# Batches 2 to 7 without TensorE transposes in a windowed attention and gated MLP kernel

## The chip, the cores and the metric

The kernel runs on one core of a Trainium2 chip. The metric is the time of one execution on the device in microseconds, lower is better. The core has TensorE (PE in the profile), VectorE (DVE), ScalarE (ACT), GpSimd (POOL) and SyncE (SP), which here only issues DMAs. Matrix products go from SBUF into PSUM, which has eight banks of 128 partitions x 512 f32.

## What is computed

An attention with a causal window of 64 positions, whose output feeds a gated MLP. Eight batches, eight heads, 576 positions, 64 dimensions a head; everything comes and goes in f32:

```python
scores = scale * np.matmul(q, k.transpose(0, 1, 3, 2))          # q, k, v: (8, 8, 576, 64)
mask = (rel >= 0) & (rel < 64)                                  # rel = query - key
attn = softmax(np.where(mask, scores, -1e9))
x = np.matmul(attn, v)                                          # heads side by side: (8, 576, 512)

h = np.maximum(x @ w_in, 0.0)                                   # (8, 576, 1024)
u, v = h[..., :512], h[..., 512:]
v_n = (v - mean(v)) / np.sqrt(var(v) + 1e-06)
v_s = np.einsum('ts,bsd->btd', w_spatial, v_n) + b_spatial[None, :, None]
out = (u * v_s) @ w_out                                         # (8, 576, 512)
```

## The kernel before

Each batch is cut into small operations with a one-letter name, a batch and an index. `T` transposes q and k on PE, `S` makes scores, `P` multiplies the exponentials by v and by ones (the denominators), `V` and `U` are the two halves of `x @ w_in`, `G` is the product with `w_spatial`, `O` the one with `w_out`. `S2.1` is the scores of batch 2 for heads 2 and 3; index 4 stands everywhere for the remainder, positions 512 to 575 of all eight heads. Between them stand operations of other engines: exponentials, logarithms, relu and output copies on ACT, mask, normalisation and gating on DVE, casts to f16 on POOL and ACT.

`work()` lists all operations with what they depend on and which buffers they take. `RINGS` gives the number of buffers of each kind: `mm` is six PSUM banks shared by all products, `sc` one pair of banks for the scores of two heads, `stg` twelve staging tiles of 128 x 576 f32 into which all loads go. `plan()` lays the operations out: PE takes them in the order written out by hand in `ORDER`, the other engines and the DMA queue by due times that follow from ORDER and from the list `SHIFT`, with the durations in `COST`. What comes out is a fixed program: each engine runs its instructions in that order and waits with semaphores. All DMAs are issued by SP, in one queue.

The scores need q and k with the 64 dimensions of a head on the partitions, while in memory each position has its 64 dimensions in a row. `PATH = "LLRRRRBB"` gives each batch one of three ways to turn them:

- L (batches 0 and 1): one load of two heads, a cast, transposes of 64x64 on PE (L634), evacuation of the bank (L640).
- R (batches 2 to 5): loads of 128 positions of all heads (L664, L667, the rest in L702), casts on POOL (L677, L707), transposes of 128x128 on PE (`emit_T`, L728, L723), evacuation on DVE (L735, L737, L741). `emit_S` (L757, remainder L770) then multiplies with 64 dimensions on 64 rows of PE, four tiles of 64x64 for two heads.
- B (batches 6 and 7): loads of four heads in rows of 2304 bytes (L647), DVE transposes blocks of 32x32 in f32 (L651), and ACT and POOL cast and put the positions in order (L659). Each head lies on 32 partitions in two halves of 32 dimensions. `emit_S2` (L792) adds the two halves up in PSUM, two heads at a time.

Loads of q and k of path R move rows of 256 bytes (64 dimensions of one position of one head), but q of batch 2 rows of 1 KB (`RUN4`). Those of v move rows of 256 bytes in every batch (L681, remainder L711); POOL casts v (L691) and copies it a second time shifted by 64 positions (L696, L697). Output tiles go out through L933 and the remainders through L936.

Of the kernel before, what the change touches and what calls it, by code (L numbers as in the profile page):

```python
# [33 lines left out]
class Op:  # L34
# [11 lines left out]
WINDOW = {"PE": 0, "ACT": 27.5, "DVE": 92.1, "POOL": 361.6, "DMA": 10.0}  # L46
RINGS = dict(stg=12, tt=3, qT=2, kT=2, v16=3, qk=5, rf=1, qkr=2, sc=1, mm=6, e2=3, e2r=2, lnz=2, zinv=2,
# [10 lines left out]
    "loadL": ("DMA", 880, 3050), "DT": ("DVE", 700, 800), "castLP": ("POOL", 1240, 1340), "castLA": ("ACT", 1210, 1340), "S2": ("PE", 450, 670), "S2r": ("PE", 140, 360), "E2r": ("ACT", 320, 450),  # L58
# [31 lines left out]
U6.0 V6.0 P7.0 V6.4 S7.2 G5.4 V6.1 V6.2 S7.4a P7.1 O4.4 S7.3 U6.4 U6.3 U6.1 U6.2 S7.4b P7.2 P7.3 G6.3 G6.0 P7.4 G6.2  # L90
U7.0 G6.1 G6.4 V7.2 U7.1 U7.2 V7.4 O5.4 V7.1 O5.1 V7.0 V7.3 O5.2 O6.0 O5.0 U7.4 O6.1 O5.3 G7.0 U7.3 O6.3 G7.1 G7.3
G7.4 G7.2 O6.4 O7.4 O7.0 O7.2 O7.1 O7.3 O6.2
# [220 lines left out]

PATH = "LLRRRRBB"
RUN4 = {"q": 3, "k": 2}

CAST_P, EVAC_P, CAST_L = "PAPAPAPA", "DADADADA", "APAPAPAP"
# [668 lines left out]
```

## Time and profile before

| | |
|---|---|
| median of 3 runs | 215.63 us (215.62 to 215.91) |
| the profiled execution | 215.76 us |
| its span, first to last instruction | 213.9 us |
| PE, DVE, ACT, POOL busy | 203.4, 163.6, 164.5, 109.8 us |
| DMA queue of SP, share of 16 engines | 77.1% |
| granted PE clock | 1.00 |

Busy time is the union of an engine's instructions; PE's are pipelined, so that the mean duration of a matmul is longer than its share of the time. In the slices of the page each digit is the busy share of 1/40 of the span in tenths. The chain is the work that ended last, followed back from the end. In the stretches each row gives start and end, the length, then busy time and instructions of PE, PEld (weight loads), DVE, ACT and POOL, the granted clock, the busy share of the DMA engines and GB/s. In the groups, after the bar: busy us, mean ns of one, idle time before them and what ended it.

### The profile page before, as it was taken

The numbers are of one execution on the slowest core, as the hardware profiler recorded it, in microseconds if no ns is written. First come the engines' busy times: TensorE is split into PE (matmuls) and PEld (weight loads), VectorE is DVE, ScalarE is ACT, GpSimd is POOL, SyncE is SP. The second block draws the span as 40 slices with busy tenths as digits, with TensorE's granted clock in tenths as the row PEclk, the third lists the DMA queues.
The fourth block names the chain that finished last, engine by engine and source line by source line (L and its number), as shares of the span: only waits on it lengthen the run. The fifth ranks groups of instructions, "written<-read, shape, count | busy, mean of one in ns | idle before, by whom it ended". The sixth has DMA issues, their size and how long they took to land.

```text
span 213.9 us, 7152 instructions
## 1 busy us (share of the span) xinstructions
PE 203.4 (95%) x2921; PEld 113.6 (53%) x2921; DVE 163.6 (76%) x314; ACT 164.5 (77%) x304; POOL 109.8 (51%) x162
## 2 busy tenths in 40 slices
PE   7798989899999999999999999999989999999991
PEld 2544736446645765565664556454555655545540
DVE  6388889678987889778899999996987796546310
ACT  3488889895798589857989979999878797377242
POOL 2546549757689676879726692279992000000000
PEclk9999999999999999999999999999999999999999
DMA  6998999999999998999999999897910100013516
GB/s 181 361 259 280 384 235 239 183 218 291 249 199 208 196 180 199 204 227 203 208 275 260 246 359 356 190 298 241 252 71 8 24 21 8 3 32 140 196 42 255
DMA packets 86387, 42.69 MB, mean 200 GB/s; under 512 B 72465, under 2 KB 76561, under 8 KB 86354
## 3 DMA queue, kind: packets, MB, share of 16 engines
q1 hardware_dynamic: 86354, 42.24, 77.1%
q8 instruction: 23, 0.38, 0.8%
q14 instruction: 10, 0.08, 0.2%
HBM read 32.79 MB, written 9.44 MB: 197 GB/s over the span
## 4 chain that ended last, share of the span: by engine, by line
PE 80%; ACT 6%; DMA 5%; DVE 4%; POOL 2%; issue 1%; SPq 1%
PE pg L905 19%; PE po L918 12%; PE pv L850 12%; PE pu L888 12%; DMA spk<-in_k_dram 5%; PE z L819 4%; PE o L826 4%; PE tp L728 3%; PE sc L757 3%; DVE vn L881 3%; PE pu L892 2%; PE po L922 2%; PE pv L853 2%; PE sc_None L792 2%; POOL kp L627 1%; ACT e L776 1%
## 5 line engine op out<-in xcount | busy, mean ns | idle before, releaser
L905 PE MATMUL pg<-wspT,vn 128*128 128x64 f16 (+1 forms) x256 | 38.8, 287 | 0.7 <-DVE vn L881 0.7
L850 PE MATMUL pv<-win,x 128*128 128x512 f16 x128 | 31.6, 380 | 1.0 <-issue 1.0
L868 DVE BATCH_NORM_STATS2 st<-vs 128x6 f32<-128x512 f16 (+1 forms) x40 | 27.0, 676 | 7.0 <-ACT vs L860 5.1
L888 PE MATMUL pu<-x,win 128*128 128x512 f16 x128 | 32.0, 380 | 0.3 <-ACT win L594 0.2
L691 POOL CAST v<-sv 128x512 f16<-128x512 f32 x32 | 22.3, 699 | 18.9 <-DMA sv<-in_v_dram 18.0
L912 DVE TENSOR_TENSOR g<-pg,ru 128x512 f16<-128x512 f32 (+1 forms) x40 | 24.6, 626 | 9.4 <-PE pg L905 7.1
L776 ACT ACTIVATE e<-sc 128x1024 f16<-128x1024 f32 (+1 forms) x36 | 28.4, 817 | 3.4 <-PE sc L757 1.9
L918 PE MATMUL po<-wout,g 128*128 128x512 f16 x128 | 30.8, 380 | 0.0
L839 DVE TENSOR_TENSOR x<-o,zi 128x512 f16<-128x512 f32 (+1 forms) x40 | 24.6, 629 | 7.8 <-ACT zi L835 7.7
L928 ACT COPY ob<-po 128x512 f32<-128x512 f32 (+1 forms) x40 | 21.6, 543 | 10.5 <-PE po L918 6.3
L808 DVE TENSOR_TENSOR e<-e,mask 128x1024 f16<-128x1024 f16 x32 | 24.4, 765 | 5.8 <-ACT e L776 3.8
L898 ACT ACTIVATE ru<-pu 128x512 f32<-128x512 f32 (+1 forms) x40 | 21.7, 558 | 7.8 <-PE pu L888 5.8
L905 PEld LDWEIGHTS <-vn 128*128 128x128 f16 x256 | 16.8, 98 | 14.6 <-DVE vn L881 0.8
L860 ACT ACTIVATE vs<-pv 128x512 f16<-128x512 f32 x32 | 18.9, 602 | 6.9 <-PE pv L850 6.6
L835 ACT ACTIVATE zi<-ln 128x512 f32<-128x512 f32 (+1 forms) x40 | 22.5, 595 | 0.3
L831 ACT ACTIVATE ln<-z 128x512 f32<-128x512 f32 x32 | 18.3, 607 | 5.2 <-PE z L819 5.0
L697 POOL COPY v<-v 64x512 f16<-64x512 f16 x28 | 19.9, 710 | 1.5
L918 PEld LDWEIGHTS <-g 128*128 128x128 f16 x128 | 11.9, 98 | 13.4 <-issue 0.2
L888 PEld LDWEIGHTS <-win 128*128 128x128 f16 x128 | 11.4, 98 | 13.7 <-ACT win L594 0.7
L850 PEld LDWEIGHTS <-x 128*128 128x128 f16 x128 | 11.6, 98 | 12.8 <-issue 0.6
L905 PE MATMUL pg<-wspT,vnr 128*128 128x64 f16 (+1 forms) x64 | 17.0, 287 | 0.4 <-DVE vnr L881 0.4
L826 PEld LDWEIGHTS <-v 128*64 128x64 f16 x576 | 15.0, 112 | 4.3 <-POOL v L715 0.6
(114 smaller groups left out, 352.7 us busy)
## 6 DMA issues: line engine op xcount, KB each, us to landing
sv<-in_v_dram SPq DMA_DIRECT2D x32, 256.0 KB, 5.5
out_dram<-ob SPq DMA_DIRECT2D x32, 256.0 KB, 3.3
sk<-in_k_dram SPq DMA_DIRECT2D x16, 256.0 KB, 5.6
sq<-in_q_dram SPq DMA_DIRECT2D x16, 256.0 KB, 5.2
spk<-in_k_dram SPq DMA_DIRECT2D x8, 288.0 KB, 5.2
spq<-in_q_dram SPq DMA_DIRECT2D x8, 288.0 KB, 5.6
slk<-in_k_dram SPq DMA_DIRECT2D x8, 288.0 KB, 4.5
slq<-in_q_dram SPq DMA_DIRECT2D x8, 288.0 KB, 5.8
```

Of the source, the lines that this page charges most:

```text
L691: self.nc.gpsimd.tensor_copy(v16[:, 0, n, :, :], s[:, 0:512].rearrange("c (h d) -> c h d", h=8))
L776: self.nc.scalar.activation(to, of, AF.Exp, bias=0.0, scale=0.125)
L808: self.nc.vector.tensor_tensor(e2[:, :, :], e2[:, :, :], m, ALU.min)
L826: mm(o[64 * h:64 * h + 64, 64 * u:64 * u + 64], vt, e2[:, h, 64 * u:64 * u + 64], start=True, stop=True)
L835: self.nc.scalar.activation(t, self.t.pop(("lnz", b, s)), AF.Exp, bias=0.0, scale=-1.0)
L839: self.nc.vector.tensor_tensor(x[:, :], self.t.pop(("oz", b, s))[0], self.t.pop(("zinv", b, s)), ALU.mult)
L850: mm(pv[:, :], self.t["x", b, r][:, 128 * j:128 * j + 128], w[:, r, :], start=(r == 0), stop=(r == 3))
L868: self.nc.vector.bn_stats(st[0:n, :], self.t["vs", b, j][:, :])
L888: mm(pu[:, :], w[:, r, 128 * m:128 * m + 128], self.t["x", b, r][:, :], start=(r == 0), stop=(r == 3))
L905: self.nc.tensor.matmul(to, self.t["vn", b, kk][:, 128 * n:128 * n + 128], self.wspT[kk][:, 0:512] if m < 4 else self.wspT[kk][:, 512:576] ...
L912: self.nc.vector.tensor_tensor(g[:, :], self.t.pop(("pg", b, m))[:, 0:n], self.t.pop(("ru", b, m))[:, 0:n], ALU.mult)
L918: self.nc.tensor.matmul(po[:, :], self.t["g", b, r][:, 128 * j:128 * j + 128], self.wout[:, r, :], start=(r == 0), stop=(r == 3))
```

## The change

PATH becomes `"LLBBBBBB"`: batches 2 to 7 all go path B, and path B is rewritten. A load brings four heads (all 576 positions of a quarter of 32 partitions by one DMA each, four DMAs) into a tile of the new ring `wide` (128 x 1152 f32, two of them), in rows of 256 bytes, so that partition p of a head gets positions p, p + 32, and so on. The load is cast to f16 in two halves, one on ACT and one on POOL, into a tile of the ring `qk`. DVE then transposes blocks of 32x32 in f16, which leaves the positions in order in `qT` and `kT`. `emit_S4` makes the scores of four heads in one group of 64 matmuls: the four heads lie on four row groups of 32, two key blocks go to two column halves, and the two halves of the dimensions are added in PSUM. Each head's scores have a bank of their own, and the exponential of one head is one instruction (`emit_E1`), also on path L. The ring `sc` goes, and `mm` has all eight banks. ORDER, SHIFT and the plan's windows are replaced as a whole; of ORDER the last three lines are shown.

```diff
-WINDOW = {"PE": 0, "ACT": 27.5, "DVE": 92.1, "POOL": 361.6, "DMA": 10.0}
-RINGS = dict(stg=12, tt=3, qT=2, kT=2, v16=3, qk=5, rf=1, qkr=2, sc=1, mm=6, e2=3, e2r=2, lnz=2, zinv=2,
+WINDOW = {"PE": 0, "ACT": 5.2, "DVE": 15.1, "POOL": 215.9, "DMA": 10.0}
+RINGS = dict(stg=11, wide=2, qT=2, kT=2, v16=3, qk=5, rf=0, qkr=0, mm=8, e2=4, e2r=2, lnz=2, zinv=2,
...
+O5.2 U6.3 O4.0 V6.4 P7.1 U6.2 U6.1 U6.0 G5.4 P7.4 P7.2 P7.0 P7.3 O4.2 G6.2 G6.3 G6.0 V7.2 O5.3 G6.1 U6.4 V7.1 V7.3
+U7.2 U7.3 O4.4 V7.4 O5.4 O6.0 V7.0 U7.1 U7.4 O6.2 O5.0 O5.1 O6.3 G7.2 U7.0 G6.4 G7.4 G7.3 G7.1 G7.0 O7.4 O6.4 O7.3
+O7.0 O7.2 O7.1 O6.1
...
-PATH = "LLRRRRBB"
+PATH = "LLBBBBBB"
...
-                    for n in (0, 1):
-                        s, f, eng = slot("stg"), slot("tt"), CAST_L[4 * hh + 2 * "kq".index(x) + n]
-                        ld = op("loadL", lambda b=b, x=x, hh=hh, n=n: E.load_rows(b, x, hh, n), takes=[s])
-                        d = op("DT", ..., [ld] + tts.get(x, []), takes=[f], frees=[s])
-                        ready[hh].append(op("castL" + eng, ..., [d] + first.get(x, []),
+                    s, f, deps = slot("wide"), slot("qk"), []
+                    ld = op("loadB", lambda b=b, x=x, hh=hh: E.load_rows(b, x, hh), takes=[s])
+                    for n in (0, 1):
+                        eng = CAST_L[4 * hh + 2 * "kq".index(x) + n]
+                        c = op("cast_L" + eng, ..., [ld] + deps, takes=[] if n else [f], frees=[s] + [f] * n)
+                        d = op("DT", ..., [c] + first.get(x, []), takes=[] if hh or n else [qkT[x]], frees=[f, qkT[x]])
+                        ready[hh].append(d)
...
-                sc = [slot("mm"), slot("mm")] if r else [slot("sc")]
+                sc = [slot("mm"), slot("mm")]
...
+            elif s4 in (0, 2):
+                four = [slot("mm") for _ in range(4)]
+                so = op("S4", lambda b=b, s=s4: E.emit_S4(b, s), ready[s4 // 2], ..., takes=four, ...)
+            if not r:
+                if path == "B":
+                    sc = four[2 * (s4 % 2):2 * (s4 % 2) + 2]
+                exs = []
+                for h in (0, 1):
+                    exs.append(op("E", lambda b=b, s=s4, h=h: E.emit_E1(b, s, h), [so] + exs, takes=[] if h else [e2], frees=[sc[h]]))
...
-    def load_rows(self, b, x, hh, n):
-        s = self.t["rows", b, x, hh, n] = self.tile("stg", [128, 576], self.f32, f"sl{x}{b}_{hh}{n}")
-        self.nc.sync.dma_start(s[:, :], self.src[x][b, 4 * hh:4 * hh + 4, :, :].rearrange("h (p j) d -> (h p) (j d)", j=18)[:, 576 * n:576 * n + 576])
+    def load_rows(self, b, x, hh):
+        s = self.t["rows", b, x, hh] = self.tile("wide", [128, 1152], self.f32, f"sl{x}{b}_{hh}")
+        for h in range(4):
+            self.nc.sync.dma_start(s[32 * h:32 * h + 32, :].rearrange("p (j d) -> p j d", j=18),
+                                   self.src[x][b, 4 * hh + h, :, :].rearrange("(j p) d -> p j d", p=32))
+
+    def cast_rows(self, b, x, hh, n, eng):
+        if not n:
+            self.t["tt", b, x, hh] = self.tile("qk", [128, 2, 18, 32], self.f16, f"tt{x}{b}_{hh}")
+        copy = self.nc.scalar.copy if eng == "A" else self.nc.gpsimd.tensor_copy
+        copy(self.t["tt", b, x, hh][:, :, 9 * n:9 * n + 9, :],
+             self.t["rows", b, x, hh][:, 576 * n:576 * n + 576].rearrange("c (j e p) -> c e j p", j=9, e=2))
 
     def transpose_rows(self, b, x, hh, n):
...
+        self.nc.vector.transpose(self.t[x, b][:, hh, :, 288 * n:288 * n + 288],
+                                 self.t["tt", b, x, hh][:, :, 9 * n:9 * n + 9, :].rearrange("c e j p -> c e (j p)"))
...
+    def emit_E1(self, b, s, h):
...
+        self.nc.scalar.activation(self.t["e2", b, s][:, h, :], sc[h][:, :], AF.Exp, bias=0.0, scale=0.125)
...
+    def halves(self, b, hh, d, to, key, c0, c1, shift=0):
+
+        q, k, r = self.t["q", b], self.t["k", b], 64 * (key % 2)
+        return [lambda e=e: self.nc.tensor.matmul(to[r:r + 64, c0 + shift:c1 + shift], k[d:d + 32, hh, e, 64 * key:64 * key + 64],
+                                                  q[d:d + 32, hh, e, c0:c1], start=(e == 0), stop=(e == 1)) for e in (0, 1)]
+
+    def emit_S4(self, b, s):
+        sc = [self.mm(f"sc{b}_{s + h // 2}_{h % 2}") for h in range(4)]
+        self.t["sc", b, s], self.t["sc", b, s + 1] = sc[0:2], sc[2:4]
+        for key in range(0, 8, 2):
+            runs = [self.halves(b, s // 2, 32 * h, sc[h], n, 0 if n == 1 else 64 * n, min(512, 64 * n + 128)) for n in (key, key + 1) for h in range(4)]
+            for e in (0, 1):
+                for run in runs:
+                    run[e]()
```

`emit_S2` and `emit_E2` are left for the remainder alone, which takes two banks of `mm` each time and has one exponential for each bank.

More of the change, by code (lines that the diff above doesn't have):

```diff
@@ L90 @@
[L90 to L92 removed]
+warmup T0.3k T0.1k T0.2k T0.0q T0.0k T0.1q S0.1 T0.2q T0.3q S0.0 S0.2 T1.1k S0.4 S0.3 P0.1 P0.2 P0.4 P0.3 T1.0q T1.0k
+P0.0 T1.2k V0.3 T1.1q V0.4 V0.1 S1.1 U0.4 V0.2 S1.0 T1.2q V0.0 U0.0 T1.3k U0.1 W1 W0 W4 T1.3q W2 U0.2 U0.3 S1.3 W3
@@ L749, in emit_S @@
         if s < 4:
-            sc = self.t["sc", b, s, None] = self.tile("sc", [128, 2, 512], self.f32, f"sc{b}_{s}", True)
+            sc = self.t["sc", b, s] = [self.mm(f"sc{b}_{s}_{h}") for h in (0, 1)]
             q, k = self.qk_of(b, s)
@@ L770, in emit_S @@
                     mm(sc[h][r:r + 64, 64 * p:64 * p + 64], k8[d, :] if r == 0 else k[d, 448:512], q[d, :], start=True, stop=True)
-    def emit_E(self, b, s):
-        e2 = self.t["e2", b, s] = self.tile("e2" if s < 4 else "e2r", [128, 2, 512 if s < 4 else 256], self.f16, f"e2_{b}_{s}")
-        sc = self.t.pop(("sc", b, s, None))
-        for to, of in [(e2[:, :, :], sc[:, :, :])] if s < 4 else [(e2[:, h, :], sc[h][:, 0:256]) for h in (0, 1)]:
-            self.nc.scalar.activation(to, of, AF.Exp, bias=0.0, scale=0.125)
@@ L779, in emit_S2 @@
-    def emit_S2(self, b, s, g):
-        sc = self.t["sc", b, s, g] = self.tile("sc", [128, 2, 512], self.f32, f"sc{b}_{s}_{g}", True)
-        q, k = self.t["q", b], self.t["k", b]
-        if s < 4:
-            parts = [(2 * s, kap, max(0 if kap == 1 else 64 * kap, 0), min(512, 64 * kap + 128), 0) for kap in range(8)]
-        else:
-            parts = [(2 * g + 4 * hh, kap, 512, 576, 64 * hh - 512) for hh in (0, 1) for kap in (8, 7)]
-        for two in range(0, len(parts), 2):
-            for e in (0, 1):
-                for head, kap, c0, c1, shift in parts[two:two + 2]:
-                    r = 64 * (kap % 2)
-                    for h in (0, 1):
-                        hh, d = (head + h) // 4, 32 * ((head + h) % 4)
-                        self.nc.tensor.matmul(sc[r:r + 64, h, c0 + shift:c1 + shift], k[d:d + 32, hh, e, 64 * kap:64 * kap + 64],
-                                              q[d:d + 32, hh, e, c0:c1], start=(e == 0), stop=(e == 1))
@@ L795, in emit_E2 @@
-    def emit_E2(self, b, s, g):
-        if ("e2", b, s) not in self.t:
-            self.t["e2", b, s] = self.tile("e2" if s < 4 else "e2r", [128, 2, 512 if s < 4 else 256], self.f16, f"e2_{b}_{s}")
-        e2, sc = self.t["e2", b, s], self.t.pop(("sc", b, s, g))
-        to, of = e2[:, :, :], sc[:, :, :]
-        if s == 4:
-            to = e2[:, :, :].rearrange("p h (f g c) -> p h f g c", f=2, g=2)[:, :, :, g, :]
-            of = sc[:, :, 0:128].rearrange("p h (f c) -> p h f c", f=2)
-        self.nc.scalar.activation(to, of, AF.Exp, bias=0.0, scale=0.125)
+    def emit_E1(self, b, s, h):
+        if not h:
+            self.t["e2", b, s] = self.tile("e2", [128, 2, 512], self.f16, f"e2_{b}_{s}")
+        sc = self.t["sc", b, s] if not h else self.t.pop(("sc", b, s))
+        self.nc.scalar.activation(self.t["e2", b, s][:, h, :], sc[h][:, :], AF.Exp, bias=0.0, scale=0.125)
@@ new lines, in emit_E @@
+    def emit_E(self, b, s):
+        e2 = self.t["e2", b, s] = self.tile("e2r", [128, 2, 256], self.f16, f"e2_{b}_{s}")
+        sc = self.t.pop(("sc", b, s))
+        for h in (0, 1):
+            self.nc.scalar.activation(e2[:, h, :], sc[h][:, 0:256], AF.Exp, bias=0.0, scale=0.125)
+    def halves(self, b, hh, d, to, key, c0, c1, shift=0):
+        q, k, r = self.t["q", b], self.t["k", b], 64 * (key % 2)
+        return [lambda e=e: self.nc.tensor.matmul(to[r:r + 64, c0 + shift:c1 + shift], k[d:d + 32, hh, e, 64 * key:64 * key + 64],
+                                                  q[d:d + 32, hh, e, c0:c1], start=(e == 0), stop=(e == 1)) for e in (0, 1)]
@@ new lines, in emit_S4 @@
+    def emit_S4(self, b, s):
[6 more added lines that the diff above has]
+                    run[e]()
+    def emit_S2(self, b, s, g):
+        sc = self.t["sc", b, s, g] = [self.mm(f"sc{b}_{s}_{g}{h}") for h in (0, 1)]
+        for hh in (0, 1):
+            runs = [self.halves(b, hh, 32 * (2 * g + h), sc[h], n, 512, 576, 64 * hh - 512) for n in (8, 7) for h in (0, 1)]
+            for e in (0, 1):
+                for run in runs:
+                    run[e]()
@@ L805, in emit_M @@
+    def emit_E2(self, b, s, g):
+        if not g:
+            self.t["e2", b, s] = self.tile("e2r", [128, 2, 256], self.f16, f"e2_{b}_{s}")
+        sc = self.t.pop(("sc", b, s, g))
+        for h in (0, 1):
+            self.nc.scalar.activation(self.t["e2", b, s][:, h, :].rearrange("p (f g c) -> p f g c", f=2, g=2)[:, :, g, :],
+                                      sc[h][:, 0:128].rearrange("p (f c) -> p f c", f=2), AF.Exp, bias=0.0, scale=0.125)
     def emit_M(self, b, s):
```

57 lines of the change are left out of this document (24 added, 33 removed), and 172 rows, old and new, of tables (COST, SHIFT).

## The prediction

> **What bounds the kernel now.** I read the page first (shares, slices, chain), then the chain in order of time, PE's timeline, the groups of the other engines, and the stretches and issues of the DMA. From the page:
>
> ```profile
> span 213.9 us, 7152 instructions
> ...
> PE 203.4 (95%) x2921; PEld 113.6 (53%) x2921; DVE 163.6 (76%) x314; ACT 164.5 (77%) x304; POOL 109.8 (51%) x162
> ...
> PE   7798989899999999999999999999989999999991
> ...
> DMA  6998999999999998999999999897910100013516
> ...
> PE 80%; ACT 6%; DMA 5%; DVE 4%; POOL 2%; issue 1%; SPq 1%
> ```
>
> PE is full from the eighth slice (about 42 us) to the end, and the chain is PE work: what leaves PE there leaves the time. But the DMA row is as full for 29 slices (155 us) and then empty: the loads fill the DMA engines until the last one has landed. So there are two bounds side by side, and the change moves them in opposite directions.
>
> The profiled execution took 215.76 us, 1.9 us more than its span and 0.13 us over the median of 215.63; I sum against 215.76 and give the result as a time. A difference under 0.2% (0.43 us) counts as none.
>
> **PE: what goes and what comes.** The chain in order of time gives the pitch of each operation, that is, what it costs when PE is full:
>
> ```profile
> 109.99 1.34 PE tp L728 x24
> ...
> 115.64 0.35 PE sc L757 x16
> 115.99 0.97 PE po L918 x4
> 116.96 0.86 PE pv L850 x4
> 117.82 1.08 PE pg L905 x5
> ...
> 164.08 0.57 PE sc_None L792 x27
> 164.65 1.19 PE pg L905 x5
> ...
> 183.89 1.66 PE pg L905 x25
> ...
> 195.28 0.47 PE pu L892 x16
> ...
> 209.56 0.58 ACT ob L928
> ```
>
> and PE's timeline the three small ones:
>
> ```profile
> 95.91 0.39 PE L723 MATMUL tp<-id,rf 128*128 128x128 f16 x4
> 96.14 1.03 PE L918 MATMUL po<-wout,g 128*128 128x512 f16 x4
> ...
> 158.61 0.32 PE L792 MATMUL sc<-qT,kT 32*64 32x64 f16 x16
> 158.85 0.41 PE L819 MATMUL z<-e,ones 128*64 128x512 f16 x2
> ...
> 159.34 0.39 PE L819 MATMUL z<-e,ones 128*64 128x512 f16 x2
> ```
>
> Transposes: eight of them cost 1.34/3 = 0.447 us, the four of the last rows 96.14 - 95.91 = 0.23. A batch of path R has 4 x 0.447 + 0.23 = 2.02, and four such batches go: 8.1 us. ORDER of the new kernel holds no T2 to T7, so this part cannot fail to happen.
>
> Scores of path R: 16 matmuls in 0.35, and 0.11 more on the group behind them (0.97 against 0.86), where the tile shape changes back: 0.46. The sixteen of the last rows I price by L792, 158.85 - 158.61 = 0.24, with 0.11 behind: 0.35. A batch: 4 x 0.46 + 0.35 = 2.19. Path B now: 32 matmuls in 0.57, with 0.11 behind (1.19 against 1.08): 0.68. A batch: 4 x 0.68 + 2 x 0.35 = 3.42. In the new kernel emit_S4 issues 64 matmuls for two score groups, on eight tiles of 32x64 in place of four. The trace has no eight tiles at once. If they run abreast, 64 matmuls take as many passes as 32 on four tiles: 0.68. If only four run at once, the bare part (0.57 - 0.11 = 0.46) doubles: 1.14. I take 0.68: sixteen matmuls of 64 columns took 0.24 with the shape change in it, so issue can follow, and the four heads go to four different banks, as the two of before go to two. A batch is then 2 x 0.68 + 0.70 = 2.06 (2.98 at the other end): 0.13 less than R, 1.36 less than B.
>
> PE sum: 8.1 + 4 x 0.13 + 2 x 1.36 = 11.3 us less (5.8 at the other end). **PE alone gives 204.5** (210.0).
>
> The rule against it: the Trainium skill ("TensorE: Matmul & The Clock Gate", section "Wait — 56ns, not 53.3ns?") states that matmuls never start less than about 25 ns apart. By it an S4 takes 1.6 us and the time is near 218, slower. This trace disagrees: 16 in 0.24 us is 15 ns apart at most.
>
> **DVE, ACT, POOL.**
>
> ```profile
> L737 DVE COPY qk<-tp 128x1024 f16<-128x1024 f16 x12 | 7.8, 677 | 0.3 <-PE tp L728 0.3
> L651 DVE STREAM_TRANSPOSE ttk<-slk 128x576 f32<-128x576 f32 x8 | 6.1, 756 | 0.0
> ...
> L735 DVE COPY qk<-tp 128x512 f16<-128x512 f16 x4 | 2.7, 672 | 0.1
> ...
> L737 DVE COPY qk<-tp 128x512 f16<-128x512 f16 x4 | 1.7, 414 | 0.0
> L741 DVE COPY qkr<-tp 128x512 f16<-128x512 f16 x4 | 1.6, 407 | 0.0
> ```
>
> ```profile
> L776 ACT ACTIVATE e<-sc 128x1024 f16<-128x1024 f32 x24 | 24.7, 1030 | 2.2 <-PE sc L757 1.9 <-PE o L826 0.3
> ...
> L898 ACT ACTIVATE ru<-pu 128x512 f32<-128x512 f32 x32 | 19.0, 600 | 5.8 <-PE pu L888 5.8
> ...
> L659 ACT CAST qT<-ttq 128x576 f16<-128x576 f32 x4 | 4.9, 1228 | 0.0
> ...
> L776 ACT ACTIVATE e<-sc 128x256 f16<-128x256 f32 x12 | 4.0, 392 | 1.2 <-PE sc L770 1.2
> ...
> L627 ACT CAST qp<-spq 128x576 f16<-128x576 f32 x4 | 2.7, 670 | 5.1 <-DMA spq<-in_q_dram 5.0
> ```
>
> DVE loses the evacuations of four batches (7.8 + 2.7 + 1.7 + 1.6 = 13.8 us) and gets 32 more block transposes. In f16 they are not in the trace; between the short f16 copy (0.41) and the f32 transpose (0.756) I take 0.75, since the element count is the same: +24. DVE: 163.6 + 10 = 174 (163 at the low end).
>
> ACT gets 16 more casts and does the 8 old ones in a plain order, 0.67 in place of 1.228: +10.7 - 4.5. Each of 32 exponentials becomes two halves, 2 x 0.60 for 1.03: +5.4, less the overlap of neighbours. The remainders become four small ones for two of 0.39: an estimate of 0.3 each (half of 0.39 and a fixed part), +0.4 a batch, +2.4. ACT: 164.5 + 13.5 = 178. POOL gives up half of its q and k casts and its old strided ones.
>
> So ACT and DVE would be 88 and 86% busy in 202 us, off the bound if their work comes in time. What the changes queue: a cast of ACT that waits for a load holds up every activation behind it, and so the banks that PE needs; S4 waits for four free banks, and all of PE stands behind it. I cost that at nothing: four banks are read out in 4 x 0.6 = 2.4 us, and the other four cover four groups of 0.86, 3.4 us. Without that cover each of the 12 S4 waits for one pair of halves, 2 x 0.6 = 1.2 us, 14 us in all.
>
> **DMA: what it costs.** The bytes stay. Rows of 2304 bytes (q and k of batches 6 and 7) and of 1 KB (q of batch 2) become rows of 256 bytes, as k, q and v of batches 3 to 5 have them now.
>
> ```profile
> 60.00:70.00 10.00, 10.00 (x147) 5.42 (x138) 8.07 (x14) 8.55 (x14) 8.69 (x11) 1.00 1.10 198
> 70.00:80.00 10.00, 10.00 (x182) 6.75 (x180) 8.70 (x15) 6.95 (x16) 6.74 (x12) 1.00 0.97 197
> ...
> 90.00:100.00 10.00, 10.00 (x160) 6.56 (x158) 7.97 (x14) 5.68 (x11) 8.30 (x13) 1.00 1.09 214
> ...
> 120.00:130.00 10.00, 10.00 (x133) 5.69 (x132) 9.79 (x21) 8.40 (x16) 7.66 (x10) 1.00 1.00 315
> ```
>
> ```profile
> 35.61 0.76 SPq L702 DMA_DIRECT2D sr<-in_q_dram  x1
> ...
> 150.62 0.57 SPq L681 DMA_DIRECT2D sv<-in_v_dram  x1
> ```
>
> ```profile
> sv<-in_v_dram SPq DMA_DIRECT2D x32, 256.0 KB, 5.5
> ```
>
> The last columns are GB/s: 197 to 214 where 256-byte rows move, 315 where longer rows are among them. Loads of batch 2 begin at 35.6 us. From there to the last v of batch 7 go 21.2 MB of q, k and v, and 6.8 MB of wout and of the stores that ORDER puts ahead of P7.1. New kernel: 21.2 MB at 198 or 214 is 107 or 99 us, 6.8 MB at 315 is 22; end 165 or 157. Old kernel, the same way at 198 (5.8 MB of the loads at 315): 153. Its last load was issued at 150.6 and takes 5.5, 156: the sum holds, 3 us short. So v of batch 7 lands at 160 to 168, and with its cast and copies on POOL, 0.7 each,
>
> ```profile
> L697 POOL COPY v<-v 64x512 f16<-64x512 f16 x28 | 19.9, 710 | 1.5
> ```
>
> P7.1 can start at 162 to 170.
>
> When would PE want it? Behind P7.1 in ORDER stand 23 groups of four matmuls (0.86), 8 of five (1.08), 3 G remainders (1.66 - 1.08 = 0.58), 7 other remainders (0.47), P7 (4 at 159.34 - 158.85 = 0.49 and a rest of 0.3), some 14 shape changes of 0.11, and 213.9 - 209.56 = 4.3 us of tail: 41 us. With a span of 204.5 - 1.9 = 202.6, P7.1 is due at 161. **The loads are 1 to 9 us late, the time 205.5 to 213.5.** I take 209, near the middle: the old kernel as a whole fits the 198, while the row at 214 shows that such rows can go faster.
>
> **Rivals.**
>
> Slower: the quarter loads set the pace. Each 590 KB load becomes four DMAs of 32 partitions, 96 in all, into only two wide buffers.
>
> ```profile
> L681 SPq DMA_DIRECT2D sv<-in_v_dram x32: 368/575/3107, 1.7 to 150.6; - x32
> ```
>
> ```profile
> L711 SPq DMA_DIRECT2D srv<-in_v_dram x8: 596/670/1259, 14.1 to 149.9; - x8
> ```
>
> A DMA of 64 partitions with half the bytes keeps SP's queue longer (0.60 us at least) than a full one (0.37). A quarter load has 0.74 us at 198 GB/s. At 0.9 each, 96 x 0.16 = 15 us more: 209 + 15 = 224. A buffer is held for about 3 us of issue, 5.5 of landing and two casts of 0.67, 10 us; two buffers then give a batch in 20 us, and each us that a cast comes later costs 2 a batch, 12 in all: 221. Meanwhile v loads and stores stand behind the waiting load in SP's queue. It decides from 7 us beyond the forecast, 0.07 us on each DMA. Against it: at 0.6 the queue has room. 216 to 235; chance 0.27.
>
> The Trainium skill ("SBUF — State Buffer", section "Door 1: The DMA port swizzle") says that 32 partitions reach 8 of 16 ports and gives 189 GB/s for them. By it q and k (14.2 MB) take 3.4 us longer than at 198; no run here shows it.
>
> Four tiles at once, not eight: PE gives 210.0, PE then asks for P7.1 later than most loads come: 210 to 213, chance 0.06. By the rule of 25 ns, 218: 0.02, for the trace speaks against it.
>
> ACT sets the pace: 178 us of work in order, with casts that wait for DMA at its head. If PE waits 0.5 us for it at each of 24 casts, 12 us on 204.5: 216 to 220, chance 0.05. Against it: batches 6 and 7 have as many casts on ACT today, at 1.228 each, and PE's row is full there.
>
> **How the numbers follow.** Forecast 209 (204.5 to 213.5): 0.51. Four tiles: 0.06. Loads later still, 213.5 to 215.3: 0.05. Within 0.2%: 0.04. Slower 0.34: quarter loads 0.27, ACT 0.05, the rule 0.02. Faster 0.62. Range: a start that goes better or worse by 2 us sets 202.5 below; above it reaches into the loads' rival to 222, and some 0.15 is left out.
>
> **What would show it.** Right: no tp of batches 2 to 7; 64 score matmuls in 0.57 us before the next group; transposes near 0.75; the DMA row full to about 165 us; PE idle of 4 to 5 us ahead of late scores or P of batches 5 to 7. Wrong: S4 over 0.9; quarter loads over 0.8 us each in SP's queue; PE idle spread over all batches behind DVE's transposes or ACT. A DMA row that falls empty well before 160 would show that the loads were never near the bound.

## The result and the profile after

The changed kernel takes 234.88 us (median of 4 runs, 234.26 to 237.38) where the kernel before takes 215.77 (215.62 to 216.74) beside it: a ratio of 1.0897, 95% interval 1.0812 to 1.0982. The forecast of 209.0 and its range up to 222.0 are missed by far. The profiled execution took 234.93 us, its span is 233.2. (Here and below a median takes in all runs; a ratio leaves out those more than 1.5% above the fastest of their kernel.)

From the page of the changed kernel, the lines that answer to those of before:

```profile
span 233.2 us, 7594 instructions
...
PE 200.0 (86%) x3085; PEld 106.2 (46%) x3085; DVE 171.8 (74%) x322; ACT 169.7 (73%) x364; POOL 91.4 (39%) x142
...
PE   7758599978896975797999779997978999999993
...
DMA  6999999999999999999999999999989002112516
...
q1 hardware_dynamic: 106450, 42.24, 91.1%
...
PE 29%; DMA 24%; SPq 18%; DVE 10%; POOL 7%; ACT 5%; issue 5%; POOLq 0%; ACTq 0%
```

PE has holes everywhere until slice 31, and is full only behind it. The DMA row is full for 31 slices of 5.8 us, up to 181 us, where it was full for 29 slices of 5.3 us, up to 155. The chain was PE for 80%; now loads and SP's queue (24 + 18%) hold more of it than PE. So the loads seem to set the pace from batch 2 to batch 7; the experiments below test that.

The stretch from 70 to 100 us, busy time of the engines, granted clock, DMA share and GB/s, first before, then after:

```profile
70.00:100.00 30.00, 30.00 (x445) 18.17 (x443) 25.43 (x46) 22.44 (x45) 22.02 (x34) 1.00 0.97 203
```

```profile
70.00:100.00 30.00, 22.52 (x371) 11.79 (x364) 23.69 (x43) 22.42 (x50) 14.28 (x19) 1.00 1.23 168
```

The DMA engines were busier (1.23 against 0.97; above 1 the times of the packets add up to more than the engines had, so some overlapped) and moved less, 168 GB/s against 203. PE stood idle for 7.5 of 30 us. Who waits for the loads, from the view of waits (us in total, times, longest):

```profile
POOL v L708 <- DMA sv<-in_v_dram: 30.9, 20, 6.2
...
POOL ttk L669 <- DMA slk<-in_k_dram: 13.6, 6, 4.1
ACT ttk L669 <- DMA slk<-in_k_dram: 13.2, 9, 2.3
...
ACT ttq L669 <- DMA slq<-in_q_dram: 11.1, 7, 3.0
POOL ttq L669 <- DMA slq<-in_q_dram: 10.8, 5, 3.9
```

The first line says little: POOL waits as long for v (30.6 us) in the run y3 below, which takes 218 us. It is the waits of the casts of q and k that differ, 48.7 us here and 7.4 there.

The last two v were issued from 175.01 us on (before, the last at 150.62), by the queue's timeline:

```profile
175.01 1.20 SPq L698 DMA_DIRECT2D sv<-in_v_dram  x2
```

The parts that were forecast for the engines, from PE's timeline and the groups:

```profile
63.11 0.38 PE L933 MATMUL pg<-wspT,vnr 128*128 128x512 f16 x1
63.42 0.76 PE L805 MATMUL sc<-qT,kT 32*64 32x128 f16 x64
64.11 1.04 PE L946 MATMUL po<-wout,g 128*128 128x512 f16 x4
```

```profile
L793 ACT ACTIVATE e<-sc 128x512 f16<-128x512 f32 x64 | 35.0, 615 | 1.7 <-PE sc L774 1.6
...
L675 DVE STREAM_TRANSPOSE qT<-ttq 128x576 f16<-128x576 f16 x24 | 18.1, 763 | 7.6 <-ACT ttq L669 4.8
...
L675 DVE STREAM_TRANSPOSE kT<-ttk 128x576 f16<-128x576 f16 x24 | 17.5, 754 | 7.0 <-ACT ttk L669 4.9
```

64 score matmuls hold PE for 64.11 - 63.42 = 0.69 us, and the one G matmul ahead of them, 0.215 when PE is full, for 0.31: 0.79 in all. The eight tiles run nearly abreast. The f16 transposes take 0.76 us. DVE's work is about what was forecast (171.8 us for 174) and ACT's is less (169.7 for 178). PE's fell by 3.4 us only, from 203.4 to 200.0, where 11.3 was forecast; the run v6 below shows more of it. But PE is not what binds here: it stands idle for 33 us.

### The profile page after: what moved, and what is told of

The parts are those of the page before. It is cut to its first block, busy times and chain, and to the rows that moved or that the text cites. A ratio compares the mean times of both kernels' runs of the same rounds, so it can differ in the third digit from the quotient of the medians.

```text
span 233.2 us, 7594 instructions
## 1 busy us (share of the span) xinstructions
PE 200.0 (86%) x3085; PEld 106.2 (46%) x3085; DVE 171.8 (74%) x322; ACT 169.7 (73%) x364; POOL 91.4 (39%) x142
## 4 chain that ended last, share of the span: by engine, by line
PE 29%; DMA 24%; SPq 18%; DVE 10%; POOL 7%; ACT 5%; issue 5%; POOLq 0%; ACTq 0%
SPq L662 13%; DMA slk<-in_k_dram 7%; PE pg L933 7%; PE po L946 6%; DMA slq<-in_q_dram 6%; DMA sv<-in_v_dram 6%; PE pv L878 5%; PE pu L916 4%; DVE e L836 3%; DMA spq<-in_q_dram 2%; DMA spk<-in_k_dram 2%; SPq L698 2%; DVE x L867 2%; POOL ttq L669 2%; DVE qT L675 2%
## 5 line engine op out<-in xcount | busy, mean ns | idle before, releaser
L933 PE MATMUL pg<-wspT,vn 128*128 128x64 f16 (+1 forms) x256 | 39.3, 291 | 0.0
L793 ACT ACTIVATE e<-sc 128x512 f16<-128x512 f32 x64 | 35.0, 615 | 1.7 <-PE sc L774 1.6
L708 POOL CAST v<-sv 128x512 f16<-128x512 f32 x32 | 21.0, 657 | 31.5 <-DMA sv<-in_v_dram 30.9
L946 PE MATMUL po<-wout,g 128*128 128x512 f16 x128 | 31.4, 385 | 0.0
L836 DVE TENSOR_TENSOR e<-e,mask 128x1024 f16<-128x1024 f16 x32 | 25.1, 805 | 1.0 <-ACT e L793 0.9
L675 DVE STREAM_TRANSPOSE qT<-ttq 128x576 f16<-128x576 f16 x24 | 18.1, 763 | 7.6 <-ACT ttq L669 4.8
L675 DVE STREAM_TRANSPOSE kT<-ttk 128x576 f16<-128x576 f16 x24 | 17.5, 754 | 7.0 <-ACT ttk L669 4.9
L805 PE MATMUL sc<-qT,kT 32*64 32x128 f16 (+2 forms) x960 | 15.1, 220 | 8.4 <-ACT e L793 2.4
L854 PE MATMUL o<-e,v 128*64 128x64 f16 x576 | 16.2, 196 | 3.7 <-POOL v L732 3.5
L805 PEld LDWEIGHTS <-kT 32*64 32x64 f16 x960 | 11.3, 103 | 16.9 <-issue 15.2
```

The costliest lines, as they stand in the source:

```text
L675: self.nc.vector.transpose(self.t[x, b][:, hh, :, 288 * n:288 * n + 288], self.t["tt", b, x, hh][:, :, 9 * n:9 * n + 9, :].rearrange("c e ...
L793: self.nc.scalar.activation(self.t["e2", b, s][:, h, :], sc[h][:, :], AF.Exp, bias=0.0, scale=0.125)
L805: return [lambda e=e: self.nc.tensor.matmul(to[r:r + 64, c0 + shift:c1 + shift], k[d:d + 32, hh, e, 64 * key:64 * key + 64], q[d:d + 32, h ...
L836: self.nc.vector.tensor_tensor(e2[:, :, :], e2[:, :, :], m, ALU.min)
L933: self.nc.tensor.matmul(to, self.t["vn", b, kk][:, 128 * n:128 * n + 128], self.wspT[kk][:, 0:512] if m < 4 else self.wspT[kk][:, 512:576] ...
L946: self.nc.tensor.matmul(po[:, :], self.t["g", b, r][:, 128 * j:128 * j + 128], self.wout[:, r, :], start=(r == 0), stop=(r == 3))
```

## Experiments

A quarter load differs from the earlier loads in three ways: short rows (256 bytes), 32 partitions, and four DMAs into one of two buffers. The theory after the result is that the loads lack rate; rivals are the two buffers, SP's queue, and DVE or ACT.

**Rows and cut, with the token order put back by DVE.** Each of three kernels changes the loads and lets DVE write with a stride of 36 bytes.

```diff
-        for h in range(4):
-            self.nc.sync.dma_start(s[32 * h:32 * h + 32, :].rearrange("p (j d) -> p j d", j=18),
-                                   self.src[x][b, 4 * hh + h, :, :].rearrange("(j p) d -> p j d", p=32))
+        # x1: one DMA, 128 partitions x 4608 bytes
+        self.nc.sync.dma_start(s[:, :], self.src[x][b, 4 * hh:4 * hh + 4, :, :].rearrange("h (p j) d -> (h p) (j d)", j=18))
+        # x2: t = 0, 1: two DMAs, 128 partitions x 9 rows of 256 bytes ("h (p j t) d -> (h p) t j d")
+        # x3: h = 0 to 3: four DMAs, 32 partitions x 4608 bytes ("(p j) d -> p (j d)")
```

> The changed kernel (234.9 us, PE idle from 40 to 180 us, DMA row full to 175 us, 161 to 206 GB/s) with one edit: each 590 KB load is one DMA of 128 partitions with rows of 4608 bytes, and DVE's transposes write the positions with a stride, so that they end in the same order. Program order, buffers and all other work as in the changed kernel. All theories that put the loss in the loads: the DMA row empties near 150 us, PE is full again from about 42 us on, and the time falls to what PE alone allows, 205 to 209. Theory that the loss lies in the order, the two wide buffers or the waits of the casts: stays over 225. If the strided transpose costs more than 0.9 us (0.76 now), that is seen in its group.

> As x1, but with rows of 256 bytes (each second position), in two DMAs of 128 partitions and 9 rows a partition for each load. Quarter theory (cutting a load into DMAs of 32 partitions slows it): the 256-byte rows then go at the 198 to 214 GB/s that batches 3 to 5 had before, time 206 to 214. Row theory (256-byte rows are the price, whatever the cut): as slow as the changed kernel, 230 to 236.

> As x1 with rows of 4608 bytes, but in four DMAs of 32 partitions for each load, as the changed kernel has them. Quarter theory: still slow, 222 to 236. Row theory: as x1 within 2 us, 205 to 210. If a quarter DMA costs the queue about 0.6 us whatever it carries, 0.6 x 4 = 2.4 us a load is under the pace of PE and the time is 205 to 210 too.

Measured: 293.41, 292.33 and 293.97 us; ratios 1.3593 (1.3546 to 1.3640), 1.3569 (1.3474 to 1.3663) and 1.3571 (1.3473 to 1.3669). All the same, so the loads cannot be what binds. From the groups of the first:

```profile
L673 DVE STREAM_TRANSPOSE qT<-ttq 128x576 f16<-128x576 f16 x24 | 62.9, 2691 | 0.0
```

The transpose with the stride takes 2.69 us in place of 0.76; DVE is busy for 249 us and sets the time. These three do not decide about the loads.

**A third wide buffer.** Paid for with two of the seven output tiles (`{"wide": 3, "ob": 5}`).

> The changed kernel with three wide buffers in place of two (and five output tiles in place of seven, for room); plan, order and loads stay as they are. Buffer theory (a load waits for a wide buffer, and v waits behind it): the waits of SP for the casts of the wide tiles go (some 10 us in the trace) and the time falls by 5 to 12, to 223 to 230. If the DMA engines are full anyway: within 2 us of 234.9.

Measured 248.07 us, ratio 1.1511 (1.1448 to 1.1573): slower still, and for a reason of its own, since ACT now waits for output tiles. From its view of waits:

```profile
ACT ob L956 <- DMA out_dram<-ob: 26.3, 4, 9.8
```

So the four were made again without these side costs: the same loads with DVE writing as in the changed kernel, and the third buffer paid for with a staging tile and the warm-up's scratch.

> x1 to x3 were held up by DVE: the strided transposes took 2.70 us in place of 0.76. So here the transposes write as in the changed kernel, and the positions of q and k stay in the order in which the rows come (this is the part of the computation that changes; all instructions and their sizes are those of the changed kernel). Loads: one DMA of 128 partitions, rows of 4608 bytes. By the sum for PE, with S4 at its measured 0.79 in place of 0.68: 206 if nothing else is late; loads as cause: 205 to 209. Order, casts or waits as cause: over 222.

> As y1, but rows of 256 bytes in two DMAs of 128 partitions. Share of the DMA queue times span: 165 us before, 212 in the changed kernel, 178 in x2. Quarter theory: 34 of the 47 us of DMA time more go with the cut, the time is 206 to 214. Row theory: 226 to 236. PE's full stretch tells: if DMA still binds, its row is full to 155 us or later.

> As y1, with rows of 4608 bytes in four DMAs of 32 partitions. x3 has 167 us of DMA time (x1: 151). Row theory and quarter theory both allow 206 to 212 here, since 167 is what the kernel before has; if the cut alone is enough to lose, by the issue of 96 DMAs or by head-of-line waits, it is over 220.

> x4 lost by its five output tiles (ACT waited 26 us for stores). Here three wide buffers, seven output tiles, ten staging tiles in place of eleven and a smaller scratch for the warm-up products; plan, order and loads of the changed kernel. Buffer theory: 5 to 12 us less than 234.9. DMA engines full anyway: within 2 us.

| loads of q and k | us | ratio (95%) | DMA share |
|---|---|---|---|
| y1: one DMA, 4608-byte rows | 216.66 | 0.9957 (0.9904 to 1.0010) | 69.3% |
| y2: two DMAs of 128 partitions, 256-byte rows | 219.36 | 1.0159 (1.0088 to 1.0230) | 77.9% |
| y3: four of 32 partitions, 4608-byte rows | 218.22 | 1.0101 (1.0048 to 1.0154) | 77.7% |
| y4: as changed, three wide buffers | 234.35 | 1.0861 (1.0786 to 1.0936) | 90.4% |

The loads are the cause: changing them alone brings back 16 to 20 us by the ratios, of the 19 lost. (In y1 to y3 the positions of q and k stay in the order of the load, so these are not versions to use.) The buffers are not: a third one brings nothing that can be told from the spread of the runs. And neither the short rows (y2) nor the cut in quarters (y3) does it by itself; only both together fill the DMA engines. What in the cut matters was still open: the partitions, the number of DMAs, or the order of the rows in memory.

**Partitions, count or order.** All with pieces of 256 bytes; v3, v4, v5 and v6 keep the pieces apart by a gap of 4 bytes in the tile, and take the room from the warm-up's scratch.

```diff
+        # v1: h, t = 0, 1: four DMAs, 64 partitions x 9 pieces      v3: h = 0 to 3: four, 32 partitions x 18 pieces, one stretch of memory each
+        # v4: h = 0, 1: two DMAs, 64 partitions x 18 pieces         v5: four DMAs, 128 partitions x 5, 4, 5, 4 pieces
+        # v6: one DMA, 128 partitions x 18 pieces
+            self.nc.sync.dma_start(s[:, :].rearrange("p (j d) -> p j d", d=65)[:, j0:j1, 0:64],
+                                   self.src[x][b, 4 * hh:4 * hh + 4, :, :].rearrange("h (p j) d -> (h p) j d", j=18)[:, j0:j1, :])
+        # p1: the changed kernel with
+        for h in (0, 2, 1, 3):
```

> Each tile of q or k (128 x 1152) is fetched by four DMAs of 64 partitions x 9 rows of 256 bytes, where the changed kernel has four of 32 partitions x 18 rows of 256 bytes: as many DMAs, bytes and rows in each, twice the partitions. (The positions of q and k stay in the order of the load, so the scores are taken between other tokens.) Theory A, what costs is that 32 partitions take 256-byte rows: with 64 partitions the DMA share falls from 91% to about 80%, 219 to 224 us. Theory B, what costs is many small DMAs of short rows however they are cut: 91% and 232 to 237 us. Theory C, what costs is that neighbouring 256-byte rows of memory go to different partitions in the changed kernel (here each partition reads from a stretch of its own): 218 to 222 us.

> Quarters as in the changed kernel, four DMAs of 32 partitions x 18 pieces of 256 bytes, but each partition's 18 pieces are one stretch of 4608 bytes in memory; in the tile each piece is set apart by 4 bytes, so that they stay 18 pieces. (The positions of q and k stay in the order of the load, so the scores are taken between other tokens.) Theory A (32 partitions with 256-byte rows): as the changed kernel, DMA share about 90%, 230 to 237 us. Theory B (many small DMAs of short rows): the same, 230 to 237 us. Theory C (the order in memory): as the run with quarters of long rows, 78% and 217 to 221 us.

> The changed kernel with the four quarter DMAs of a tile issued in the order 0, 2, 1, 3, so that DMAs that follow each other write partitions 0 to 31, 64 to 95, 32 to 63, 96 to 127. If a quarter is slow because the DMAs beside it in the queue write the same half of the partitions (a rule of the Trainium skill, SBUF - State Buffer, Door 1, has the lower and the upper 64 partitions behind different ports), the alternation brings the time to 222 to 230 us. If each DMA of 32 partitions and short rows is slow by itself (theory A without ports, B or C), nothing changes: 233 to 237 us.

> Each tile of q or k by two DMAs of 64 partitions x 18 pieces of 256 bytes (1152 pieces a DMA; pieces of one partition lie together in memory and stand 4 bytes apart in the tile). Positions of q and k stay in the order of the load, so the scores are taken between other tokens. The run with two DMAs of 128 partitions x 9 pieces, also 1152 a DMA, took 219.4 us with 78% DMA share; the run with four of 64 x 9 took 233.1 with 88%. Theory B (the number of DMAs with short pieces): as two DMAs, 218 to 222 us, about 78%. Theory A (partitions of a DMA): as the four DMAs of 64 partitions, 230 to 235 us, about 88%.

> Each tile by four DMAs of all 128 partitions x 5, 4, 5 and 4 pieces of 256 bytes (512 to 640 pieces a DMA). Positions of q and k stay in the order of the load, so the scores are taken between other tokens. Theory B (the number of DMAs with short pieces): as four DMAs of 64 or 32 partitions, 230 to 236 us, 88 to 91%. Theory A (partitions of a DMA): as the two DMAs of 128 partitions, 218 to 222 us, about 78%.

> Each tile by one DMA of 128 partitions x 18 pieces of 256 bytes (2304 pieces). Positions of q and k stay in the order of the load, so the scores are taken between other tokens. Theory B: as fast as two DMAs or faster, 215 to 219 us, 74 to 78% DMA share, so that short pieces alone cost next to nothing against the 216.7 us of one DMA with long rows. Theory A: the same, since all partitions are written. If short pieces cost by themselves and two DMAs were fast for another reason: 221 us or more.

| pieces of 256 bytes | us | ratio (95%) | DMA share |
|---|---|---|---|
| v1: 4 DMAs, 64 partitions | 233.07 | 1.0804 (1.0734 to 1.0874) | 88.5% |
| v3: 4 DMAs, 32 partitions, memory in a row | 235.84 | 1.0919 (1.0834 to 1.1004) | 89.2% |
| v4: 2 DMAs, 64 partitions | 235.85 | 1.0988 (1.0923 to 1.1052) | 96.4% |
| v5: 4 DMAs, 128 partitions | 217.69 | 1.0103 (1.0034 to 1.0172) | 78.5% |
| v6: 1 DMA, 128 partitions | 217.81 | 1.0145 (1.0094 to 1.0196) | 82.2% |
| p1: as changed, quarters 0, 2, 1, 3 | 229.03 | 1.0652 (1.0598 to 1.0705) | 88.0% |

After v1 and v3 the count of DMAs looked like the cause (theory B); v4 and v5 turned that round, each within 1 us of what theory A (the partitions of a DMA) expects. Two DMAs of 64 partitions are as slow as four, four of 128 as fast as one: what counts is whether a DMA with short pieces writes all 128 partitions. The order in memory does nothing that shows (v3). The same stretch as above, for v4 and then for v5:

```profile
70.00:100.00 30.00, 23.94 (x361) 12.00 (x361) 24.52 (x44) 22.48 (x51) 13.59 (x20) 0.94 1.22 162
```

```profile
70.00:100.00 30.00, 27.48 (x481) 14.70 (x476) 29.45 (x53) 26.84 (x59) 16.62 (x26) 1.00 0.99 206
```

The loads of both have the same bytes and pieces; in v4 the engines are busier (1.22 against 0.99) and move 162 GB/s in place of 206.

The Trainium skill ("SBUF — State Buffer", section "Door 1: The DMA port swizzle") says that partitions 0 to 63 reach no more ports than 0 to 31, 8 of 16, and only 128 partitions reach all. The runs agree on the first point, 64 partitions being as slow as 32 (235.85 and 233.07 against 234.88). They add that the row length decides whether it costs anything: with 4608-byte rows quarters took 218.22 us, by the ratios 1.4% more than one DMA (1.0101 against 0.9957). Alternating the halves (p1) took 5.9 us off 234.88, a third of what the full width gives; 229.03 lies in the range that was expected from the ports, 222 to 230, and outside the 233 to 237 expected if each DMA is slow by itself. The Trainium skill ("SBUF — State Buffer", section "Can I just issue two DMAs to hit both halves?") has two DMAs on the two halves at only +6% over one. The trace of p1 is in line with that: its stretch from 70 to 100 us moved 178 GB/s against 168, 6% more. The ports themselves are in no trace: that they are the reason is the Trainium skill's account, and one DMA over 32 partitions of each half (32 to 95), which would show it, was not tried.

**Versions that keep the token order.** The full-width loads above leave the positions in another order. Two ways that keep the token order:

```diff
+        # z1: one DMA of 4608-byte rows; DVE transposes in f32; all 48 casts on POOL put the tokens in order
+        # c1: order 0, 2, 1, 3, and for q two tokens a piece; q is read with a stride for the scores
+                                   self.src[x][b, 4 * hh + h, :, :].rearrange("(j p t) d -> p j (t d)", p=32, t=t))
+                                                  q[d:d + 32, hh, e, c0:c1].rearrange("d (w t p) -> d w p t", t=2, p=32), ...)
```

> The changed kernel's scores, ring and order, but q and k of batches 2 to 7 come by one DMA of 128 partitions x 4608-byte rows for each tile, are transposed in f32 (0.75 us each as in the kernel before) and then cast by POOL with the reordering that the kernel before has in its batches of that kind (1.21 us each). Three tiles are added for the transposed f32, one of the 11 staging tiles and one of the 5 q/k tiles given up, and the due times of loads, transposes and casts are no longer shifted. The loads are those of the run of 216.7 us. ACT loses 24 casts of 0.67 us (170 to 154 us), POOL goes from 91 to 91 - 17 + 48 x 1.21 = 132 us. Theory 'ACT and DVE near their limit hold the run with long rows at 217': 211 to 214 us. Theory 'the start holds it, whatever ACT does': 216 to 218 us. If POOL's longer chain (transpose, then 1.2 us of cast in line) delays the scores: 220 us or more.

> The changed kernel with the quarters in the order 0, 2, 1, 3 (229.0 us by itself) and, for q alone, pieces of 512 bytes, two tokens each: the token order is put back where q is read for the scores, with a stride (k, the loaded operand, stays as it is). The short pieces of q and k cost the DMA engines 212 - 168 = 44 us by the runs with quarters of short and of long rows; q's half of the pieces becomes half as many, so 11 us of DMA time less. Theory B and theory A alike: 221 to 227 us and about 83% DMA share, if the strided reading costs PE nothing. If it does (the score groups of 0.79 us become 1 us or more): 227 to 231 us.

z1: 236.81 us, ratio 1.1018 (1.0967 to 1.1068). That is in the open range of 220 or more, but not by the way named there: PE waits only 0.8 us for POOL's casts of q. The DMA engines are at 63.9%; the chain is DVE for 39%, and DVE's masking takes 945 ns where y1 has 782. That POOL's long casts beside it are the reason is not shown. From z1's groups:

```profile
L832 DVE TENSOR_TENSOR e<-e,mask 128x1024 f16<-128x1024 f16 x32 | 29.6, 945 | 2.7 <-ACT e L789 2.4
```

z1 also drops the shifts of the due times, so that transposes go ahead of masking; how the loss divides was not tried. c1: 226.49 us, ratio 1.0549 (1.0477 to 1.0622). This is the range for a strided reading that costs nothing (221 to 227), but the trace shows the other case: a score group of 64 takes 1.12 us in place of 0.69, and for 1 us or more 227 to 231 was expected. So the hit is partly luck. The widest score matmuls went from 252 ns to 351, the scores of batches 2 to 7 as a whole from 23.1 to 31.2 us. From PE's groups by shape, p1 and then c1:

```profile
L805 PE MATMUL sc<-qT,kT 32*64 32x192 f16 x96 | 4.4, 252 | 0.0
```

```profile
L806 PE MATMUL sc<-qT,kT 32*64 32x192 f16 x96 | 7.0, 351 | 0.0
```

**What holds the rest.** With the loads repaired five kernels stand at 217 to 219 us, and PE's work alone was forecast at 204.5. Two kernels built on y1: `CAST_L = "PPPPPPPP"`, and `emit_M` left out for batches 2 to 7.

> The run with one DMA of long rows for each tile (216.7 us; positions of q and k in the order of the load, so the scores are taken between other tokens), with all 48 casts of q and k on POOL where 24 were on ACT: ACT 170 - 24 x 0.683 = 154 us, POOL 91 + 24 x 0.76 = 109 us, DVE the same. Theory 'ACT near its limit in 50 to 160 us holds what is left above PE's floor of 206 us': 211 to 214 us. Theory 'DVE holds it' or 'the first 50 us hold it': 215 to 218 us. If POOL's casts slow DVE beside them (as in the run with 48 reordering casts on POOL, where the masking grew from 782 to 945 ns): 218 to 222 us.

> The same run with one DMA of long rows for each tile, with the masking of the scores left out in batches 2 to 7: DVE 168 - 24 x 0.782 - 6 x 0.568 = 146 us, and P waits for ACT's exponential alone. Theory 'DVE, busy 9.8 to 10 of 10 us in 50 to 120 us, holds the middle of the run': the some 6 us of PE's idle time between 50 and 160 us go, 209 to 212 us. Theory 'the first 50 us hold it all': 215 to 218 us. Theory 'ACT holds it': 214 to 217 us.

e1: 224.01 us, ratio 1.0323 (1.0260 to 1.0387), slower; ACT fell to 159.2 us (154 expected) and that bought nothing. Its masking did not grow (750 ns), so the reason given in the expectation is not shown. PE waits 5.4 us for the masking there and 2.4 for transposes of k, against 0.2 and nothing in y1; why DVE comes later stays open. e2: 212.95 us, ratio 0.9891 (0.9840 to 0.9942) against y1's 0.9957 (0.9904 to 1.0010): less than 1% better, and the intervals overlap. It is between the expectations, above 209 to 212 and below 214. The first 50 and the next 110 us, of before, v6 and e2:

```profile
0.00:50.00 50.00, 44.51 (x790) 24.64 (x791) 36.91 (x73) 38.51 (x67) 30.09 (x52) 1.00 1.00 262
50.00:160.00 110.00, 109.34 (x1542) 62.56 (x1542) 98.16 (x184) 92.39 (x171) 77.68 (x109) 1.00 0.96 234
```

```profile
0.00:50.00 50.00, 40.15 (x697) 22.07 (x698) 34.25 (x69) 35.86 (x71) 26.67 (x46) 0.93 0.99 252
50.00:160.00 110.00, 104.66 (x1780) 55.33 (x1779) 104.01 (x193) 100.56 (x221) 58.72 (x89) 1.00 1.02 220
```

```profile
0.00:50.00 50.00, 40.25 (x710) 21.87 (x712) 34.21 (x70) 36.61 (x72) 27.36 (x47) 0.93 0.93 263
50.00:160.00 110.00, 107.19 (x1831) 57.18 (x1825) 93.41 (x173) 101.33 (x225) 58.51 (x95) 1.00 0.84 229
```

The second of these stretches in y1, which has e2's loads:

```profile
50.00:160.00 110.00, 104.78 (x1796) 55.91 (x1794) 105.16 (x194) 100.06 (x222) 60.94 (x90) 1.00 0.82 224
```

In the first 50 us v6 does 4.4 us less PE work than before, at a clock of 0.93; in the next 110 us 4.7 less, where DVE is busy for 104 of 110. Without the masking PE's idle time there falls from 5.3 us (v6; 5.2 in y1) to 2.8. So about half of the loss in the middle goes with the masking; whether DVE's load or the longer way from S to P holds it was not separated.

The start is a loss of its own: e2 keeps the masking of batches 0 and 1 and could not change it. What PE waits for there is in the view of waits, before and then v6:

```profile
PE tp_3k L634 <- POOL kp L627: 1.2, 1, 1.2
```

```profile
PE pv L877 <- DVE x L866: 4.0, 4, 2.2
...
PE tp_3k L648 <- POOL kp L641: 2.5, 1, 2.5
...
PE o L846 <- DVE e L835: 1.8, 1, 1.8
PE tp_k L648 <- POOL kp L641: 1.7, 1, 1.7
```

PE waits 4.2 us for POOL's casts of k of path L, 1.2 before, and POOL itself waits 5.3 us for those loads, 3.2 before. It waits 1.8 us for DVE's masking and, once, 2.2 us for x (the attention's output, scaled on DVE), which it did not before. So at the start, too, it is loads, casts and DVE that come later under the new order. No run changed the order alone; in z1, which drops the shifts but also has other casts, PE waits 0.6 us for DVE in the first 50 us and is busy for 43.9. No version with the reference's token order beats the kernel before.

## Why the prediction was wrong

**The step that failed is the rate of the loads.** "New kernel: 21.2 MB at 198 or 214" took the rate of the old loads of batches 3 to 5, because the rows have the same length. But those write 128 partitions with each DMA (64 for the remainders), and the new ones 32. With the 168 GB/s of the stretch after, the same sum gives 35.6 + 21.2/0.168 + 22 = 184 us for the end of the loads; the last v was issued at 175.0 to 176.2, and with the 5.8 us that such a load takes to land that is 182. The sum for the end of the loads was right, the rate in it was not: the row's bytes were compared, the partitions were not.

The step behind it failed as well: P7.1 did not wait for the last v. POOL was done with v at 182.6 us, and PE came to P7.1 at 192.8:

```profile
181.96 0.61 POOL L732 CAST v<-srv 64x512 f16<-64x512 f32 x1
```

```profile
192.76 0.38 PE L847 MATMUL z<-e,ones 128*64 128x512 f16 x2
```

By then PE was behind with its own work, from the waits in the batches before. From P7.1 to the end of the span it is 40.4 us, as forecast (41).

**The rival "the quarter loads set the pace"** (216 to 235, chance 0.27) is what came, at its upper end. Two of its three mechanisms fall. The two wide buffers, priced at 221, cost nothing that y4 shows. SP's queue did take 0.66 and 0.76 us for a quarter load (median; q and k), more than the 0.6 taken and less than the 0.8 that was named as the sign against the forecast, so that the rival came without its sign; but four DMAs for each tile cost nothing when they are 128 partitions wide (v5). What it priced at 3.4 us by the Trainium skill's 189 GB/s, the partitions, was the cause: with short rows 17 us (234.9 against 217.7), with long rows about 3 (1.4% by the ratios).

**PE idle "of 4 to 5 us ahead of late scores or P of batches 5 to 7"**: wrong. The loads bind from batch 2 on, the idle time lies in every stretch (7.5 of 30 us between 70 and 100), and behind the last load PE runs full.

**PE's sum** held in kind. The changed kernel's own trace shows 3.4 us less PE work, with PE waiting in every stretch. v6, with its loads repaired, shows 196.5 us of PE work for 203.4, 6.9 less where 11.3 was forecast. S4 at 0.79 in place of 0.68 is 12 x 0.11 = 1.3 of the difference; a clock of 0.93 over 40 us of work is an estimated 2.8. With both, 11.0. Eight tiles do run abreast, and the Trainium skill's rule of 25 ns, the prediction's rival, is contradicted again: 64 matmuls in 0.69 us are 10.8 ns apart. The term put at nothing, S4 waiting for four free banks, stayed small once the loads were repaired: between 50 and 160 us of v6 PE waited 0.2 us for ACT's exponentials there.

**DVE and ACT**: 171.8 and 169.7 us for 174 and 178. The transposes were right (0.76 for 0.75), ACT was priced 8 us too high. That they are off the bound no longer holds once the loads are repaired: in v6 DVE is busy for 9.5 of 10 us between 50 and 160, and DVE ended 3.6 us of PE's waits there.

**The start** was given "better or worse by 2 us". The new program leaves PE idle for 4.4 us more in the first 50 us, at the lower clock. With these 4.4 and the estimated 2.8 in the prediction's own sum, PE alone would have given 209 to 212 in place of 204.5.

## What to carry to other kernels

Before a rate is carried from one load to another, compare the partitions that each DMA writes and not only the length of its rows: between 70 and 100 us, kernels with short pieces to 32 or 64 partitions moved 159 to 168 GB/s (v3, v4 and the changed kernel), with short pieces to 128 partitions 185 to 207 (y2, v5, v6). In this kernel a load cut by quarter cost little with long rows, and so did 256-byte pieces over the full width; avoid the two together, and if they must be, try to alternate the lower and the upper half. And when a change also replaces the order of the start, price the first stretch by itself.

## What the runs showed of the hardware

- A DVE block transpose of 128x576 f16 takes 0.76 us with contiguous output and 2.69 with elements 36 bytes apart.
- Loads by DMAs of 256-byte pieces to 64 partitions are as slow as to 32 (235.85 and 233.07 us against 234.88); the number of DMAs for a tile (one or four, 128 partitions) makes no difference that these runs resolve (217.8 and 217.7 us).
- A matmul on a 32x64 tile whose moving operand is read with a stride of 64 bytes takes longer, 351 ns against 252 for 192 columns.
- PE's granted clock over the first 50 us was 1.00 in the kernel before, where PE is busy for 44.5 of them, and 0.90 to 0.97 in the others, where it is mostly busy for 40 to 41; but z1, with 43.9, has 0.93, so that the busy time alone does not set it.
